# Sinkhorn-sorted attention into a squared-ReLU feed-forward layer: transposes in one bank for each moving engine, 1e-9 as a ninth row, and an earlier key move as the gate of w_in

## The chip, the cores and the metric

The kernel runs on one core of one Trainium2 chip. The time is device microseconds (us) of one execution, and the median over several executions is what counts. Before the change it is 230.9 us, the median of 6 runs that lie between 229.33 and 233.6 us.

A core has five engines with an instruction queue each, which run side by side and wait for one another through semaphores: PE (TensorE, matrix products and transposes; "PEld" is its loading of the stationary operand), DVE (VectorE), ACT (ScalarE), POOL (GpSimd) and SP (SyncE, which here only issues transfers). POOL issues transfers too. Each engine takes its own instructions strictly in the order of the program.

## The reference

The inputs are q, k and v (4 batches, 8 heads, 768 tokens, 64 dimensions), a sort net of 8x8 numbers for every batch and head, and a feed-forward layer's w_in (512x2048) and w_out (2048x512) with scalars s and b.

```python
P = sort_net
for _ in range(5):
    P = exp(P - max(P, axis=-1))
    P = P / (sum(P, axis=-1) + 1e-09)
    P = P / (sum(P, axis=-2) + 1e-09)
k_sorted = einsum('bhij,bhjcd->bhicd', P, k_blocks)   # v_sorted likewise
attn = softmax(q_blocks @ k_sorted_blocks^T / 8)      # within a block of 96 tokens
x = (attn @ v_sorted_blocks) as (3072 tokens, 512)
out = (s * relu(x @ w_in)**2 + b) @ w_out             # (3072, 512), fp32
```

So the five rounds of normalizing (the Sinkhorn stage) work on 32 matrices of 8x8, each of the 8 blocks of keys and values becomes a weighted sum of all 8, attention runs inside blocks, and then comes the layer that holds nearly all of the arithmetic.

## The kernel before, in words

**Tiling.** Tokens are handled in 8 groups of 384 (half a batch, four blocks of 96). Every group goes through `ffn1` (x by w_in, 16 column blocks of 128 taken two at a time, then ReLU on ACT and a square on DVE into the tile `gt`) and `ffn2` (`gt` by w_out). The order of all engines' work is written out by hand: a call of `ffn1` or `ffn2` is given `slots`, a dictionary that says which small pieces of the next group's attention are put between which of its matmuls. Negative slot numbers belong to `ahead`: with ahead=3 the first halves of the sums of column blocks 0, 1 and 2 (`part(i, (0, 1))`, L418 on, which need only the first two of the four 128-row slices of x) are done first, and slot i-3 runs just before the i-th of them. Slot ("pre", 1) runs on PE after the second half of block 1's sum.

**Start.** The Sinkhorn stage (L185 to L205) keeps its 32 matrices in the tile `sn`, one per partition, and is a chain of small DVE instructions with one exponential on ACT in every round: row sums (L195), reciprocal, product (L197), column sums (L200), in the first round alone 1e-9 added to them (L203, from the small tile `eps`, filled at L110), reciprocal (L204), product (L205). PE meanwhile does matmuls on zeros (`warm`, L157). Then `spread_p`, `take_p` and `build_pd` turn the result into weights for batch 0, and three `k_piece` (L249) and four `v_piece` (L300) sort the keys and values of batch 0: PE writes a piece into PSUM, and ACT ("A") or DVE ("D") moves it to SBUF by `evac` (L241). The three key pieces go into disjoint columns of `KS[0]`, by ACT, DVE and ACT.

**The gate of the weights.** w_in and w_out are loaded by POOL (`load_w`, L126, called at L473). In front of it stands a POOL copy of one column (L472) from the third key piece's part of `KS[0]` to the tile `ones`, which makes POOL wait until ACT has moved that piece. `load_w` issues six pieces of w_in at L131 (first columns 0 to 511 and 512 to 1023 of row slices 0 and 1, then columns 0 to 511 of slices 2 and 3), the second half of batch 0's queries (four transfers, L99), two pieces (columns 512 to 1023 of slices 2 and 3), eight more, and four of w_out (L147). POOL then does fills (L496 to L502), loads two scalars and, in `loads(1)` (L517), batch 1's keys, values and queries (L88, L99) and reorders the values (`vp`, L171). Batch 1's first value pieces on PE (L304, in `ffn2` of group 0) need these.

**Around the transposes.** For each pair of heads, `s_piece` makes scores, `p_piece` weighs the values and normalizes them into the tile `x` (reciprocal L361, product L362 on DVE). `t_piece` (L371) transposes x on PE for two pairs of heads into `tr`, a PSUM tile of one bank, and moves it into `xt`, the right operand of `ffn1`. The letters in `eng` say who moves: "D" is DVE alone, "AD" is ACT for the first two blocks of 96 tokens and DVE for the other two. For group 0, head pairs 0 and 1 are transposed at L490 with "AD", and pairs 2 and 3 as slot -2 of `ffn1(0)` (L551) with "D". `tr` comes from the pool `psb` with two banks, which are used in turn by the `warm` matmuls, `tr`, the query transposes `tqb` (L286, `q_blocks`) and the score banks `scb` (L334).

Of the kernel before, what the change touches and what calls it, by code (L numbers as in the profile page):

```python
# [9 lines left out]
FP = mybir.dt.float32  # L10
BF = mybir.dt.bfloat16
AF = mybir.ActivationFunctionType
ALU = mybir.AluOpType
# [3 lines left out]
def spread(t, dims):  # L17

    return bass.AP(tensor=t.tensor, offset=t.offset, ap=[list(t.ap[0])] + dims)
# [3 lines left out]
def kernel(  # L23
# [12 lines left out]
    nc = tc.nc  # L36

    B, H, S, D = q.shape
    NB = sort_net.shape[-1]
    BLK = S // NB  # L40
    BH = B * H
# [4 lines left out]
    HB = NB // 2  # L46
# [6 lines left out]
    CK = 16  # L53
# [5 lines left out]
    const = ctx.enter_context(tc.tile_pool(name="const", bufs=1))  # L59
# [9 lines left out]
    psb = ctx.enter_context(tc.tile_pool(name="psb", bufs=2, space=bass.MemoryType.PSUM))  # L69
    ctx.enter_context(tc.manual_schedule())  # L70


    sn = const.tile([BH, NB, NB], FP)
    nc.sync.dma_start(out=sn, in_=sort_net.rearrange("b h i j -> (b h) i j"))
    v0f = gtp.tile([128, C2, D], FP, tag="gt", name="v0f")
    CV = C2 // 4
    for c in range(0, C2, CV):
        nc.sync.dma_start(out=v0f[:, c:c + CV, :].rearrange("p c d -> p (c d)"),
                          in_=raw[2][0][:, c * D:(c + CV) * D])
# [13 lines left out]
    def load_q(b, ns=range(NB)):  # L93

        if b not in QTOK:
            QTOK[b] = rawp.tile([BLK, NB, H, D], BF, tag="rawq", name="qtok")
        qv = q[b].rearrange("h (n t) d -> t n h d", n=NB)
        for n in ns:
            nc.gpsimd.dma_start(out=QTOK[b][:, n], in_=qv[:, n])  # L99
# [5 lines left out]
    KS = [const.tile([128, NG, 2, GAP], BF, name=f"ks{i}") for i in range(2)]  # L105
    VS = [const.tile([KR, 2 * NG, VW], BF, name=f"vs{i}") for i in range(2)]
    nc.vector.memset(VP[0][:, :, C2:GAP], 0.0)
    nc.vector.memset(KS[0][:, :, :, C2:GAP], 0.0)
    eps = const.tile([BH, NB], FP)
    nc.vector.memset(eps, 1e-9)  # L110


    ident = const.tile([128, 128], BF)
# [8 lines left out]
    ones = const.tile([128, 32], BF)  # L122
# [3 lines left out]
    def load_w():  # L126
        wiv = moe_w_in.rearrange("(a p) f -> p a f", p=128)
        fq = d_ff // 4

        def part(a, f0, f1):  # L130
            nc.gpsimd.dma_start(out=wi[:, a, f0 * fq:f1 * fq], in_=wiv[:, a, f0 * fq:f1 * fq])  # L131

        for c in (0, 1):
            for a in (0, 1):
                part(a, c, c + 1)
        for c in (0, 1):
            for a in (2, 3):
                part(a, c, c + 1)
            if c == 0:
                load_q(0, range(HB, NB))  # L140
        for c in (2, 3):
            for a in range(NHP):
                part(a, c, c + 1)
        wov = moe_w_out.rearrange("(f p) n -> p f n", p=128)
        for c in range(4):
            fs = slice(c * (NF // 4), (c + 1) * (NF // 4))
            nc.gpsimd.dma_start(out=wo[:, fs, :], in_=wov[:, fs, :])  # L147
# [17 lines left out]
    def permute(eng, b, src, cs=slice(0, C2), ds=slice(0, D)):  # L165
        o = VP[b % 2][:, ds, cs]
        i = src[:, cs, ds].rearrange("p c d -> p d c")
        if eng is nc.scalar:
            eng.copy(out=o, in_=i)
        else:  # L170
            eng.tensor_copy(out=o, in_=i)  # L171


    rstat = const.tile([BH, NB], FP)
# [5 lines left out]
            out=jsel, in_=ident.rearrange("p (h j z) -> p j h z", h=H, j=NB), axis=AX.XY, op=ALU.add),  # L180
        lambda: nc.vector.tensor_reduce(
            out=bm.rearrange("p (e z a) -> p e z a", e=2, z=2),
            in_=idv.rearrange("p a e j z -> p e z a j"), axis=AX.X, op=ALU.add),
# [3 lines left out]
                            op=ALU.subtract)  # L187
    warm(138, 128)
    for it in range(5):
        nc.scalar.activation(out=sn, in_=sn, func=AF.Exp)  # L190
        if it >= 1:
            permute(nc.scalar, 0, v0f, slice((it - 1) * CV, it * CV))
        if it in (1, 2):
            idle[it - 1]()
        nc.vector.tensor_reduce(out=rstat, in_=sn, axis=AX.X, op=ALU.add)  # L195
        nc.vector.reciprocal(out=rrec, in_=rstat)
        nc.vector.tensor_tensor(out=sn, in0=sn, in1=rrec.broadcast_to([BH, NB, NB]), op=ALU.mult)  # L197
        if it == 4:
            break
        nc.vector.tensor_reduce(out=rstat, in_=sn.rearrange("p i j -> p j i"),  # L200
                                axis=AX.X, op=ALU.add)
        if it == 0:
            nc.vector.tensor_tensor(out=rstat, in0=rstat, in1=eps, op=ALU.add)  # L203
        nc.vector.reciprocal(out=rrec, in_=rstat)  # L204
        nc.vector.tensor_tensor(out=sn, in0=sn, in1=spread(rrec, [[0, NB], list(rrec.ap[1])]),  # L205
                                op=ALU.mult)
# [34 lines left out]
    def evac(eng, out, in_):  # L241
        if eng == "A":
            nc.scalar.copy(out=out, in_=in_)  # L243
        else:
            nc.vector.tensor_copy(out=out, in_=in_)  # L245
# [3 lines left out]
    def k_piece(b, c0, eng):  # L249
        src, mov, dst = RAW["k", b], PD[b], KS[b % 2]  # L250
        ps = psa.tile([128, CK, 2, NG], FP, tag="a", name="tp")
        for c in range(CK):
            for e in range(2):
                nc.tensor.matmul(out=ps[e * 64:(e + 1) * 64, c].rearrange("p z g -> p (z g)"),  # L254
                                 lhsT=src[:, c0 + c, :],
                                 rhs=mov[:, e].rearrange("p z g -> p (z g)"),
                                 start=True, stop=True)
        evac(eng, dst[:, :, :, c0:c0 + CK], ps.rearrange("p c z g -> p g z c"))
# [112 lines left out]
    def t_piece(b, half, hp2, eng):  # L371

        x = X[b, half]
        if hp2 == 0:
            XT[b * 2 + half] = xtp.tile([128, HB, NHP, BLK], BF, tag="xt", name="xt")
        tr = psb.tile([128, 1024], BF, tag="b", name="tr")
        for hp in (hp2, hp2 + 1):
            for n in range(HB):
                c0 = (n * 2 + hp % 2) * BLK
                nc.tensor.transpose(out=tr[:, c0:c0 + BLK],  # L380
                                    in_=x[:, n, hp * 128:(hp + 1) * 128],
                                    identity=ident[0:BLK, 0:BLK])
        n = HB // len(eng)
        for i, g in enumerate(eng):
            evac(g, XT[b * 2 + half][:, i * n:(i + 1) * n, hp2:hp2 + 2, :],
                 tr[:, i * n * 2 * BLK:(i + 1) * n * 2 * BLK].rearrange("p (n a c) -> p n a c",
                                                                        n=n, a=2))

    def t_dma(b, half):
        x = X.pop((b, half))  # L390
# [7 lines left out]
    def ffn1(t, slots, ahead=0):  # L398

        gt = gtp.tile([128, NF, TG], BF, tag="gt", name="gt")  # L400
        GT[t] = gt
        xt = XT[t]
        H1 = {}

        def part(i, hpl):
            if i not in H1:
                H1[i] = psa.tile([128, 2, 512], FP, tag="a", name="hps")
            for f in range(2):
                for hp in hpl:
                    fc = (2 * i + f) * 128  # L410
                    nc.tensor.matmul(out=H1[i][:, f, 0:TG], lhsT=wi[:, hp, fc:fc + 128],  # L411
                                     rhs=xt[:, :, hp, :],
                                     start=(hp == 0), stop=(hp == NHP - 1))

        for i in range(ahead):
            for p in slots.get(i - ahead, ()):
                p()
            part(i, (0, 1))  # L418
        for i in range(NF // 2):
            part(i, (2, 3) if i < ahead else range(NHP))  # L420
            for p in slots.get(("pre", i), ()):
                p()
            rt = rtp.tile([128, 2, TG], BF, tag="rt", name="rt")
            h = H1.pop(i)[:, :, 0:TG]
            nc.scalar.activation(out=rt, in_=h, func=AF.Relu)  # L425
            nc.vector.tensor_tensor(out=gt[:, 2 * i:2 * i + 2, :], in0=rt, in1=rt, op=ALU.mult)  # L426
            for p in slots.get(i, ()):
                p()
# [38 lines left out]
    warm(3)  # L467
    k_piece(0, 0, "A")
    k_piece(0, CK, "D")
    k_piece(0, 2 * CK, "A")  # L470

    nc.gpsimd.tensor_copy(out=ones[:, 0:1], in_=KS[0][:, 0, 0, 2 * CK:2 * CK + 1])  # L472
    load_w()  # L473
    v_piece(0, 0, "D")
    v_piece(0, CK, "A")
    q_piece(0, 0, "D")
# [11 lines left out]
    warm(1)  # L488
    Z.clear()
    t_piece(0, 0, 0, "AD")  # L490
    norm2()
    p_piece(0, 0, 3)
# [50 lines left out]
    def SB(b, h, i): return lambda: s_banks(b, h, i)  # L543
    def P(b, h, i): return lambda: p_piece(b, h, i)
    def TP(b, h, i, eng): return lambda: t_piece(b, h, i, eng)
    def TD(b, h): return lambda: t_dma(b, h)
    def PDB(b): return lambda: build_pd(b)
    def QB(b, n0, eng): return lambda: q_blocks(b, n0, eng)


    ffn1(0, {-2: [TP(0, 0, 2, "D")], ("pre", 1): [QB(0, HB, "D"), QB(0, HB + 2, "D")],  # L551
             2: [SB(0, 1, 0)], 3: [SB(0, 1, 1), P(0, 1, 0)], 4: [SB(0, 1, 2), P(0, 1, 1)],
             5: [SB(0, 1, 3), P(0, 1, 2)], 6: [TP(0, 1, 0, "D"), P(0, 1, 3)]}, ahead=3)
    ffn1(1, {-2: [TP(0, 1, 2, "D")], 1: [lambda: take_p(1, B - 1, PB), PDB(1)], 4: [PDB(2)],
# [10 lines left out]
    for b in range(B):  # L565
        n = b + 1
# [48 lines left out]
```

## Time and profile before

| | us |
|---|---|
| median of the runs shown (6) | 230.9 |
| lowest and highest of them | 229.33 and 233.6 |
| the profiled execution, its own time | 229.33 |
| its span, first to last instruction | 227.6 |
| PE busy in the span | 216.8 (95%) |
| DVE, ACT, POOL busy | 124.8, 98.9, 68.0 |
| bytes moved by DMA | 25.82 MB, mean 113 GB/s |
| mean granted PE clock | 0.998 of full |

The profile is of one execution. The time of an execution is its span and 1.7 us around it (229.33 - 227.6). A row of the timeline reads: start, length (us), engine, line, operation, output <- inputs by the program's names, how many instructions were put together, and in brackets how long the engine stood idle before and what ended that wait. In the chain of waits, which is followed back from the last instruction, a row is start, length and what the end of the kernel was waiting for at that time.

### The profile page before, as it was taken

Reading aid. Unit: us, or ns where it says so; the run is one execution under the profiler, and the core shown is the slowest. Engines: PE = TensorE matmul, PEld = TensorE weight load, DVE = VectorE, ACT = ScalarE, POOL = GpSimd, SP = SyncE. Lnnn points to the kernel's source line nnn. Section 1 sums busy time; section 2 is a strip of 40 time slices with the busy share of each in tenths; the row PEclk is TensorE's granted clock in tenths of the full one; section 3 lists DMA queues with packets and bytes.
Section 4 is the critical chain, followed back from the end, with each engine's and each line's share of the span. In section 5 each row is a group of like instructions: output and inputs, shape, how many; then the busy total and the mean of one; then the engine's idle time right before and its main releaser. Section 6 shows DMA issues by size and latency. Waiting matters only on the chain.

```text
span 227.6 us, 5807 instructions
## 1 busy us (share of the span) xinstructions
PE 216.8 (95%) x2532; PEld 133.1 (58%) x2554; DVE 124.8 (55%) x224; ACT 98.9 (43%) x127; POOL 68.0 (30%) x112
## 2 busy tenths in 40 slices
PE   8997799999999999999999999999999999999993
PEld 8886456655556556665555556655556556654452
DVE  6766467553547643489556733498557544441221
ACT  4967276564324316546234236627152246650000
POOL 8419689343900009291000018390000000000000
PEclk9999999999999999999999999999999999999999
DMA  6998999999951566994111568993123340001212
GB/s 185 233 74 95 170 184 189 206 199 156 129 145 46 118 161 119 192 158 90 49 46 59 151 120 164 176 168 48 49 95 58 107 115 3 1 0 46 94 49 92
DMA packets 53930, 25.82 MB, mean 113 GB/s; under 512 B 44944, under 2 KB 49296, under 8 KB 53904
## 3 DMA queue, kind: packets, MB, share of 16 engines
q0 software_dynamic: 30864, 12.85, 46.8%
q1 hardware_dynamic: 23040, 12.59, 22.0%
q8 instruction: 20, 0.33, 0.6%
q14 instruction: 6, 0.05, 0.1%
HBM read 27.27 MB, written 6.29 MB: 147 GB/s over the span
## 4 chain that ended last, share of the span: by engine, by line
PE 72%; DMA 11%; POOL 9%; DVE 3%; issue 3%; ACT 1%; POOLq 0%
PE ops L436 32%; PE hps L411 27%; DMA rawv<-in_v_dram 7%; PE pv L354 3%; POOL wi L131 3%; DMA wi<-in_moe_w_in_dram 3%; PE tv L304 2%; PE sc L319 2%; POOL vp L171 2%; PE tp L254 2%; PE ops L449 2%; POOL wo L147 1%; ACT ks L243 1%; DMA sn<-in_sort_net_dram 1%; ACT sn L190 1%
## 5 line engine op out<-in xcount | busy, mean ns | idle before, releaser
L411 PE MATMUL hps<-xt,wi 128*128 128x384 bf16 x512 | 85.7, 326 | 0.9 <-DVE xt L245 0.7
L436 PE MATMUL ops<-wo,gt 128*128 128x512 bf16 x348 | 81.6, 379 | 2.3 <-issue 1.9
L425 ACT ACTIVATE rt<-hps 128x768 bf16<-128x768 f32 x64 | 51.1, 811 | 56.7 <-PE hps L411 49.0
L426 DVE TENSOR_TENSOR gt<-rt 128x768 bf16<-128x768 bf16 x64 | 46.8, 738 | 41.6 <-ACT rt L425 40.9
L411 PEld LDWEIGHTS <-wi 128*128 128x128 bf16 x512 | 49.4, 98 | 34.1 <-issue 1.2
L436 PEld LDWEIGHTS <-gt 128*128 128x128 bf16 x368 | 33.7, 98 | 36.9 <-issue 0.6
L457 DVE SCALAR_TENSOR_TENSOR ot<-ops,s_bc,bias 128x512 f32<-128x512 f32 (+1 forms) x25 | 18.2, 730 | 30.9 <-PE ops L436 28.4
L324 ACT ACTIVATE at<-sc 112x768 bf16<-112x768 f32 x28 | 21.3, 808 | 30.2 <-PE sc L319 30.2
L99 POOL DMA_DIRECT2D qtok<-in_q_dram x32 | 24.9, 793 | 19.4 <-DMA rawv<-in_v_dram 9.0
L362 DVE TENSOR_TENSOR x<-pv,rec 96x512 bf16<-96x512 f32 x32 | 22.0, 686 | 1.1
L245 DVE CAST vs<-tv 112x1024 bf16<-112x1024 f32 x11 | 13.3, 1223 | 10.7 <-PE tv L304 10.6
L171 POOL COPY vp<-rawv 128x384 bf16<-128x384 bf16 x24 | 18.9, 840 | 0.0
L354 PEld LDWEIGHTS <-at 112*128 112x128 bf16 (+1 forms) x256 | 12.8, 101 | 6.7 <-ACT at L324 0.6
L561 POOL COPY gate<-gt 128x1 bf16<-128x1 bf16 x2 | 0.4, 191 | 54.2 <-DVE gt L426 54.2
L354 PE MATMUL pv<-vs,at 112*128 112x66 bf16 (+1 forms) x256 | 13.9, 195 | 0.6 <-DVE vs L245 0.5
L161 PE MATMUL z<-zeros 128*128 128x128 bf16 (+1 forms) x142 | 11.0, 247 | 1.2 <-DVE zeros L102 1.0
L304 PEld LDWEIGHTS <-vp 128*64 128x64 bf16 x512 | 9.1, 112 | 3.8 <-issue 2.5
L304 PE MATMUL tv<-pd,vp 128*64 128x64 bf16 x512 | 10.4, 197 | 0.6 <-POOL vp L171 0.3
L161 PEld LDWEIGHTS <-zeros 128*128 128x128 bf16 x144 | 10.0, 111 | 1.3 <-DVE zeros L102 1.0
L243 ACT CAST ks<-tp 128x1024 bf16<-128x1024 f32 x8 | 8.1, 1012 | 4.1 <-PE tp L254 4.0
L131 POOL DMA_DIRECT2D wi<-in_moe_w_in_dram x16 | 8.6, 547 | 2.4 <-DMA wi<-in_moe_w_in_dram 1.1
L243 ACT CAST vs<-tv 112x1024 bf16<-112x1024 f32 x5 | 5.1, 1018 | 9.6 <-PE tv L304 9.6
(77 smaller groups left out, 104.2 us busy)
## 6 DMA issues: line engine op xcount, KB each, us to landing
out_dram<-ot SPq DMA_DIRECT2D x23, 256.0 KB, 2.0
qtok<-in_q_dram POOLq DMA_DIRECT2D x32, 96.0 KB, 9.7
rawk<-in_k_dram POOLq DMA_DIRECT2D x3, 768.0 KB, 6.7
rawv<-in_v_dram POOLq DMA_DIRECT2D x3, 768.0 KB, 9.9
wi<-in_moe_w_in_dram POOLq DMA_DIRECT2D x16, 128.0 KB, 5.0
wo<-in_moe_w_out_dram POOLq DMA_DIRECT2D x4, 512.0 KB, 10.5
v0f<-in_v_dram SPq DMA_DIRECT2D x4, 384.0 KB, 4.6
rawk<-in_k_dram POOLq DMA_DIRECT2D x3, 256.0 KB, 9.3
```

The costliest lines, as they stand in the source:

```text
L99: nc.gpsimd.dma_start(out=QTOK[b][:, n], in_=qv[:, n])
L161: nc.tensor.matmul(out=Z[0][:, 0:w], lhsT=zeros[:, 0:128], rhs=zeros[:, 0:w], start=True, stop=True)
L171: eng.tensor_copy(out=o, in_=i)
L304: nc.tensor.matmul(out=ps[z * GAP:(z + 1) * GAP, d, :], lhsT=VP[b % 2][:, d0 + d, :], rhs=PD[b][:, :, z, :], start=True, stop=True)
L324: nc.scalar.activation(out=at, in_=sc[0:KR, :, 0:TG], func=AF.Exp, scale=scale)
L354: nc.tensor.matmul(out=pv[0:m, e, n * VW:(n + 1) * VW], lhsT=atf[:, c0:c0 + m], rhs=VS[b % 2][:, e * NG + g0 + n, :], start=True, stop=True)
L362: nc.vector.tensor_tensor(out=x[:, :, hp * 128:(hp + 1) * 128].rearrange("p n (e d) -> p e n d", e=2), in0=pvv[:, :, :, 0:D], in1=rec.unsq ...
L411: nc.tensor.matmul(out=H1[i][:, f, 0:TG], lhsT=wi[:, hp, fc:fc + 128], rhs=xt[:, :, hp, :], start=(hp == 0), stop=(hp == NHP - 1))
L425: nc.scalar.activation(out=rt, in_=h, func=AF.Relu)
L426: nc.vector.tensor_tensor(out=gt[:, 2 * i:2 * i + 2, :], in0=rt, in1=rt, op=ALU.mult)
L436: nc.tensor.matmul(out=ops, lhsT=gt[:, f, m * 128:(m + 1) * 128], rhs=wo[:, f, :], start=(f == 0), stop=(f == NF - 1))
L457: nc.vector.scalar_tensor_tensor(out=ot[:, ns], in0=ops, scalar=s_bc, in1=BIAS[0][:, ns], op0=ALU.mult, op1=ALU.add)
```

## The change

Three edits. In the Sinkhorn stage the tile gets a ninth row `sne[:, 8, :]` of 1e-9 and `sn` becomes a view of the first eight rows; the column sums at L200 go over nine rows in four of the rounds, and the addition at L203 and the tile `eps` go. In `t_piece` every engine that moves gets a `tr` tile, and so a bank, of its own, with the transposes of its blocks written just before its move; head pairs 2 and 3 of group 0 are moved by "AD" and run as slot -1 (before the third of the first halves) where they ran as slot -2 (before the second). The POOL copy and `load_w` stand before the third key piece, and the copy reads a column of the second piece, which DVE moves.

```diff
--- before.py
+++ after.py
@@ -70,7 +70,8 @@
     ctx.enter_context(tc.manual_schedule())
 
 
-    sn = const.tile([BH, NB, NB], FP)
+    sne = const.tile([BH, NB + 1, NB], FP)
+    sn = sne[:, 0:NB, :]
     nc.sync.dma_start(out=sn, in_=sort_net.rearrange("b h i j -> (b h) i j"))
     v0f = gtp.tile([128, C2, D], FP, tag="gt", name="v0f")
     CV = C2 // 4
@@ -106,8 +107,7 @@
     VS = [const.tile([KR, 2 * NG, VW], BF, name=f"vs{i}") for i in range(2)]
     nc.vector.memset(VP[0][:, :, C2:GAP], 0.0)
     nc.vector.memset(KS[0][:, :, :, C2:GAP], 0.0)
-    eps = const.tile([BH, NB], FP)
-    nc.vector.memset(eps, 1e-9)
+    nc.vector.memset(sne[:, NB, :], 1e-9)
 
 
     ident = const.tile([128, 128], BF)
@@ -197,10 +197,8 @@
         nc.vector.tensor_tensor(out=sn, in0=sn, in1=rrec.broadcast_to([BH, NB, NB]), op=ALU.mult)
         if it == 4:
             break
-        nc.vector.tensor_reduce(out=rstat, in_=sn.rearrange("p i j -> p j i"),
+        nc.vector.tensor_reduce(out=rstat, in_=sne.rearrange("p i j -> p j i"),
                                 axis=AX.X, op=ALU.add)
-        if it == 0:
-            nc.vector.tensor_tensor(out=rstat, in0=rstat, in1=eps, op=ALU.add)
         nc.vector.reciprocal(out=rrec, in_=rstat)
         nc.vector.tensor_tensor(out=sn, in0=sn, in1=spread(rrec, [[0, NB], list(rrec.ap[1])]),
                                 op=ALU.mult)
@@ -373,18 +371,17 @@
         x = X[b, half]
         if hp2 == 0:
             XT[b * 2 + half] = xtp.tile([128, HB, NHP, BLK], BF, tag="xt", name="xt")
-        tr = psb.tile([128, 1024], BF, tag="b", name="tr")
-        for hp in (hp2, hp2 + 1):
-            for n in range(HB):
-                c0 = (n * 2 + hp % 2) * BLK
-                nc.tensor.transpose(out=tr[:, c0:c0 + BLK],
-                                    in_=x[:, n, hp * 128:(hp + 1) * 128],
-                                    identity=ident[0:BLK, 0:BLK])
         n = HB // len(eng)
         for i, g in enumerate(eng):
+            tr = psb.tile([128, 1024], BF, tag="b", name="tr")
+            for hp in (hp2, hp2 + 1):
+                for m in range(n):
+                    c0 = (m * 2 + hp % 2) * BLK
+                    nc.tensor.transpose(out=tr[:, c0:c0 + BLK],
+                                        in_=x[:, i * n + m, hp * 128:(hp + 1) * 128],
+                                        identity=ident[0:BLK, 0:BLK])
             evac(g, XT[b * 2 + half][:, i * n:(i + 1) * n, hp2:hp2 + 2, :],
-                 tr[:, i * n * 2 * BLK:(i + 1) * n * 2 * BLK].rearrange("p (n a c) -> p n a c",
-                                                                        n=n, a=2))
+                 tr[:, 0:n * 2 * BLK].rearrange("p (n a c) -> p n a c", n=n, a=2))
 
     def t_dma(b, half):
         x = X.pop((b, half))
@@ -467,10 +464,10 @@
     warm(3)
     k_piece(0, 0, "A")
     k_piece(0, CK, "D")
+
+    nc.gpsimd.tensor_copy(out=ones[:, 0:1], in_=KS[0][:, 0, 0, CK:CK + 1])
+    load_w()
     k_piece(0, 2 * CK, "A")
-
-    nc.gpsimd.tensor_copy(out=ones[:, 0:1], in_=KS[0][:, 0, 0, 2 * CK:2 * CK + 1])
-    load_w()
     v_piece(0, 0, "D")
     v_piece(0, CK, "A")
     q_piece(0, 0, "D")
@@ -548,7 +545,7 @@
     def QB(b, n0, eng): return lambda: q_blocks(b, n0, eng)
 
 
-    ffn1(0, {-2: [TP(0, 0, 2, "D")], ("pre", 1): [QB(0, HB, "D"), QB(0, HB + 2, "D")],
+    ffn1(0, {-1: [TP(0, 0, 2, "AD")], ("pre", 1): [QB(0, HB, "D"), QB(0, HB + 2, "D")],
              2: [SB(0, 1, 0)], 3: [SB(0, 1, 1), P(0, 1, 0)], 4: [SB(0, 1, 2), P(0, 1, 1)],
              5: [SB(0, 1, 3), P(0, 1, 2)], 6: [TP(0, 1, 0, "D"), P(0, 1, 3)]}, ahead=3)
     ffn1(1, {-2: [TP(0, 1, 2, "D")], 1: [lambda: take_p(1, B - 1, PB), PDB(1)], 4: [PDB(2)],
```

## The prediction

> **What bounds the kernel now.** I read the page's shares first: PE is busy for 216.8 of 227.6 us, so what PE idles, some 10.8 us, is all that a change of order can win. Then the chain of waits, to see what sets the end before PE's own work does:
>
> ```profile
> 14.66 1.02 ACT ks L243
> ...
> 15.82 0.19 POOL ones L472
> ...
> 17.39 6.04 DMA wi<-in_moe_w_in_dram
> ...
> 38.77 16.66 DMA rawv<-in_v_dram
> ...
> 56.53 4.79 POOL vp L171 x6
> 61.32 0.04 issue
> 61.36 0.44 PE tv L304 x16
> ```
>
> From 61.4 us on the chain is PE to the end (0.48 us of DVE and the last store apart). Before it, it isn't PE: from the third key move (end 15.68) it runs through POOL's gate, w_in's pieces, POOL's list of issues, batch 1's values (landed 55.44) and their reordering. So PE's work between 16 and 61 us has slack against this chain. How much: batch 1's first 96 value matmuls take from 59.33 to 61.80, 2.47 us, and the same 96 in the next batch 1.64 (at 110.17 in the chain). So 0.83 us are lost there waiting for POOL.
>
> Next, the timeline of the places that the change touches, PE, ACT and DVE together:
>
> ```profile
> 22.20 0.50 PE L380 MATMUL tr<-ident,x 96*128 96x96 bf16 x8
> 22.74 0.48 ACT L243 COPY xt<-tr 128x384 bf16<-128x384 bf16 x1 [0.33 <-PE tr L380]
> 23.25 0.36 DVE L245 COPY xt<-tr 128x384 bf16<-128x384 bf16 x1 [1.24 <-ACT xt L243]
> 23.66 0.81 PE L411 MATMUL hps<-xt,wi 128*128 128x384 bf16 x4 [0.69 <-DVE xt L245]
> 25.33 0.34 PE L380 MATMUL tr<-ident,x 96*128 96x96 bf16 x4 [0.49 <-DVE x L362]
> 28.11 0.85 PE L286 MATMUL tqb<-ident,qtok 96*128 96x96 bf16 x16
> 29.30 0.66 PE L411 MATMUL hps<-xt,wi 128*128 128x384 bf16 x3 [0.18 <-DMA wi<-in_moe_w_in_dram]
> ```
>
> DVE's half of the move begins only when ACT's has ended, and PE idles 0.69 us for it; later 0.49 us for the last product of x. But the last row matters more: PE then stands still for a w_in piece. It is the eighth; it was issued at 24.36 and took 4.9 us, so it landed at 29.26. That transfer is on the POOL chain, so whatever PE wins before 29.3 is lost again there unless the transfer moves too.
>
> **Part 1, the ninth row.**
>
> ```profile
> 3.81 0.25 DVE L200 TENSOR_REDUCE rstat<-sn 32x8 f32<-32x64 f32 x1
> 4.10 0.15 DVE L203 TENSOR_TENSOR rstat<-rstat,eps 32x8 f32<-32x8 f32 x1
> 4.29 0.19 DVE L204 RECIPROCAL rrec<-rstat 32x8 f32<-32x8 f32 x1
> ```
>
> Removing L203 takes 4.29 - 4.10 = 0.19 us out of a chain in which every instruction waits for the one before. Four column sums get 8 more elements each. No row has 72 elements; the sums over 64 and over 192 elements (0.22 us for PT of batch 0, 0.35 for PT of batches 1 to 3) give (0.35 - 0.22)/128 = 1.0 ns an element, so 8 ns, four times 0.03 us. From both sides: 0 if a short instruction's fixed cost hides them, 4 x 0.25 x 8/64 = 0.12 if the time is in proportion; I take 0.03, since the two rows bracket 72. The fill at 2.17 stays where it was. If it now had to wait for sort_net's landing (2.29) because it writes into the same tile, its 0.07 us would come on the path; its row is disjoint from what the transfer writes, so I take 0, at most 0.1. Net 0.16 us earlier, range 0 to 0.19. ACT is no bound here: a round lasts 1.76 us (4.76 to 6.52) and ACT's exponential and value copy take 1.69 of it (4.76 to 6.45). Everything after the stage moves by 0.16, PE's zero matmuls having ended at 10.63, before the stage does (11.0).
>
> **Part 2, the gate.** The second key move is a DVE row from 14.16 for 1.23 us and ends at 15.39; the third, ACT's, ends at 15.68. POOL has been idle for 7.52 us before its copy, so the copy and all behind it move by 0.29 us. Nothing is queued behind the waiting copy on POOL but these issues, and SP isn't touched. That earlier transfers start at once is seen in the one-microsecond windows (last columns: granted clock, DMA share, GB/s):
>
> ```profile
> 14.00:15.00 1.00, 0.91 (x59) 0.82 (x54) 0.84 (x1) 1.00 (x2) 0.00 (x0) 1.00 0.34 22
> 16.00:17.00 1.00, 1.00 (x35) 0.88 (x29) 0.72 (x2) 0.83 (x1) 0.71 (x3) 1.00 0.00 0
> ```
>
> The DMA engines run dry before w_in, so the whole list (w_in, queries, w_out, keys, values) begins 0.16 + 0.29 = 0.45 us earlier and, being one stream in a fixed order, should land 0.45 earlier.
>
> Two things could spoil it. First, the third key move could have to wait for POOL's copy, if reading one column of the tile blocked writing others: it would start at 15.72, not 14.66, so up to 1.06 us on ACT. Against it, ACT and DVE moved key pieces into interleaved columns of that tile at the same time (13.65 to 15.68 and 14.16 to 15.39). I take 0; PE's slack before 29.3 (below) would hide most of it. Second, a rule of the Trainium skill speaks against an earlier issue: by "SBUF — State Buffer", section "Who interferes with whom", a DVE copy in a two-port mode locks GpSimd out of a port pair that it needs to write descriptors, and GpSimd then waits for all of that instruction. The first w_in issue, before at 16.30, would come at 15.85, within the DVE value cast that ran from 15.45 to 16.68. If that blocked, the issue would come at 16.68 - 0.16 = 16.52, and the change would cost 0.22 us in place of winning 0.45. The rows say no: the six issues of 16.30 to 19.5, alongside DVE moves out of PSUM at 15.45, 16.95 and 18.39, took 0.56 to 0.58 us each, against 0.53 later with a quieter DVE. So at most 0.05 each, and those exist already. I take 0.45, between -0.22 and 0.45.
>
> **Part 3, the transposes.** The eight transposes stay, as four and four, and so do 0.48 us of ACT. DVE's move starts when the second four are done, at 22.74 beside ACT's instead of at 23.25: 0.51 earlier (0 if the two are kept apart by writing the same xt, but their parts of it are disjoint). PE's first sums start at 23.15, DVE's next products end at 23.93 and 24.77 where they ended at 24.44 and 25.28. With the second transposes moved behind two first halves, PE does 8 sums in a row at 0.173 us (16 in 2.77), waits 0.1 for the bank of the product that ends at 23.93, and comes to the transposes at about 24.65, so their 0.49 us wait falls to 0.1. Their move, 0.56 us of DVE alone, is 0.48 of ACT beside 0.36 of DVE, under the 0.7 us of the third first half. The query transposes, which began at 28.11, could begin at 27.15: PE wins 0.96 us.
>
> And it goes away at once. The last of the queries issued at 21.79 takes 6.2 us and lands at 28.0, the seventh and eighth w_in pieces at 28.6 and 29.26. Less the gate's 0.29 (on a clock that leaves out part 1), PE waits 0.2 for queries, 0.2 for the seventh and 0.3 for the eighth piece, until 28.97. So at the row that was at 29.30, PE is earlier by 0.29 + 0.16 = 0.45, the POOL chain's shift, and not by 0.96 + 0.16. The score matmuls behind it took 0.42 us to the next row (29.89 to 30.31) where the like ones take 0.27 (31.72 to 31.99), waiting for DVE's query moves, which now come earlier: 0.15 more, PE ahead by 0.60. That also is spent, at 59.33, where the values come only 0.45 earlier.
>
> **Sum.** 0.16 + 0.29 + 0 = 0.45 us on the path. The profiled execution's own 229.33 (span 227.6 and 1.7 around it) becomes 228.9. It was the fastest of the six; the same 0.45 off the median 230.9 gives 230.4. One per cent, 2.3 us, is about what a measurement of this kernel can tell from no change, its runs lying 4.3 us apart, so this forecast is "the same".
>
> **The rivals.**
> *More comes through* (0.20): the transfers land earlier by more than the gate moved, so PE keeps its 0.60 and the 0.83 us wait at 59.33 vanishes: 1.43 us off, 229.5. For it: the landing of the values is 16.66 us of shared transfer, in which a shift can grow. Against it: same list, same order, same queue.
> *The transfers hide the change* (0.12): w_out and the values come at the rate of the DMA engines and land when they did; then both PE gains wait, 230.9. For it: the DMA digits are 9 from 11 to 57 us. Against it: the windows above.
> *PE's clock drops* (0.18, slower): PE's waits for queries and w_in now lie together, about 0.7 us between 27.5 and 29. By the Trainium skill, "TensorE: Matmul & The Clock Gate", section "HAM oscillation — how this bites in real kernels", a gap that fills an idle window of about 3.4 us halves the clock. Such a window at half speed costs some 1.7 us: 230.4 + 1.7 = 232.1, two 233.8. [...]The trace is against it: from 23 to 24 us PE was busy for 0.34 us and the granted clock stayed 1.00; by the row the price is 0.
>
> **The numbers.** My forecast has 0.50; its own range is 229.1 to 231.7, from the part bounds and medians of such scattered runs. Of it I leave 0.08 to faster by over 1% (under 228.6) and 0.05 to slower by over 1% (over 233.2); of "more comes through" 0.10 and 0.01; of "hide" 0.02 and 0.01; of the clock, half, 0.09, to slower. That makes faster 0.20, same 0.64, slower 0.16. The range that leaves out two in ten reaches to both rivals: 228.4 to 232.8.
>
> **What would show it.** After, the chain should still pass from POOL's copy to the values, at about 15.4 in place of 15.8, and the values land near 55.0. ACT's and DVE's xt moves should overlap, PE's first sums start near 23.0, and PE should wait for w_in at about 28.85, longer than 0.2 us. No L203 row. I am wrong if PE no longer waits for w_in or vp, if the copy at L472 still comes at 15.8, if issues on POOL grow past 0.58 us, or if the granted clock falls below 1.00 before 62 us.

## The result and the profile after

The changed kernel took 231.40 us (median of 35 runs, 229.56 to 233.43), the kernel before 231.16 us (72 runs, 229.09 to 234.38) in the same sessions. The ratio is 1.0019, 95% interval [1.0003, 1.0035]: 0.4 us slower, where 0.45 us faster was forecast. It is within 1% of no change, as forecast, but the sign is not. (The medians are of all runs; the ratio is of the means of those runs that lie within 1.5% of the fastest of their kernel.)

The profiled execution of the changed kernel took 232.44 us, with a span of 230.7 us against 227.6. Its chain of waits (start, length, what was waited for) runs through the same places, but begins elsewhere:

```profile
2.14 7.28 DMA v0f<-in_v_dram
...
9.44 1.51 ACT vp L169
10.95 0.17 ACT sne L190
...
16.34 0.19 POOL ones L468
...
40.23 18.33 DMA rawv<-in_v_dram
...
59.66 4.75 POOL vp L171 x6
...
64.45 0.44 PE tv L302 x16
```

Two things are to be seen. The third quarter of batch 0's values (v0f) landed at 9.41; before, it landed at 7.1 (issued at 2.13, 5.0 us). ACT's cast of it stands in front of the fifth exponential, which therefore came at 10.86 and not at 9.89 (10.05 before, less the 0.16 of the ninth row). The Sinkhorn stage ended 0.80 us later than before (the first product on `pe` at 11.96, not 11.16), and POOL's copy came at 16.34, not 15.82, though the gate's own gain was there (0.28 us: DVE's key piece ended at 16.20, ACT's at 16.48). Then the stretch from that copy to the first reordering of batch 1's values (vp) took 59.66 - 16.34 = 43.32 us; before it took 56.53 - 15.82 = 40.71. The differences, 0.52 and 2.61, add up to the 3.1 us between the spans.

The sums over nine rows, in the timeline of DVE, are as forecast: 0.30 us from the first sum to the reciprocal, where it was 0.48 with the addition between.

```profile
3.80 0.27 DVE L200 TENSOR_REDUCE rstat<-sne 32x8 f32<-32x72 f32 x1
4.10 0.19 DVE L202 RECIPROCAL rrec<-rstat 32x8 f32<-32x8 f32 x1
```

The transposes, in the timelines of ACT, DVE and PE:

```profile
23.07 0.48 ACT L241 COPY xt<-tr 128x384 bf16<-128x384 bf16 x1 [0.17 <-PE tr L380]
23.29 0.36 DVE L243 COPY xt<-tr 128x384 bf16<-128x384 bf16 x1 [0.77 <-PE tr L380]
23.79 1.55 PE L408 MATMUL hps<-xt,wi 128*128 128x384 bf16 x8 [0.27 <-DVE rec L359]
25.18 0.62 PE L380 MATMUL tr<-ident,x 96*128 96x96 bf16 x8
28.85 0.34 PE L284 MATMUL tqb<-ident,qtok 96*128 96x96 bf16 x4 [0.34 <-DMA qtok<-in_q_dram]
30.39 1.13 PE L408 MATMUL hps<-xt,wi 128*128 128x384 bf16 x4 [1.20 <-DMA wi<-in_moe_w_in_dram]
```

ACT and DVE move at the same time (before, DVE waited for ACT), PE's wait ahead of the first sums is 0.27 us in place of 0.69, and the wait for x at the second transposes is gone. What PE won it gave back three rows further down: 0.34 us for queries and 1.20 for w_in.

### The profile page after: what moved, and what is told of

It is laid out like the page before. It is cut to its first block, busy times and chain, and to the rows that moved or that the text cites. A ratio compares the mean times of both kernels' runs of the same rounds, so it can differ in the third digit from the quotient of the medians.

```text
span 230.7 us, 5809 instructions
## 1 busy us (share of the span) xinstructions
PE 217.8 (94%) x2532; PEld 133.6 (58%) x2554; DVE 124.7 (54%) x223; ACT 99.5 (43%) x128; POOL 67.9 (29%) x112
## 4 chain that ended last, share of the span: by engine, by line
PE 71%; DMA 16%; POOL 7%; issue 2%; DVE 1%; ACT 1%; SPq 1%; POOLq 0%
PE ops L433 32%; PE hps L408 27%; DMA rawv<-in_v_dram 8%; DMA wi<-in_moe_w_in_dram 5%; DMA v0f<-in_v_dram 3%; PE pv L352 3%; PE tv L302 2%; PE sc L317 2%; POOL vp L171 2%; PE tp L252 2%; PE ops L446 2%; POOL wo L147 1%; POOL wi L131 1%; ACT vp L169 1%; DVE ks L243 1%
## 5 line engine op out<-in xcount | busy, mean ns | idle before, releaser
L302 PE MATMUL tv<-pd,vp 128*64 128x64 bf16 x512 | 10.7, 197 | 1.6 <-POOL vp L171 1.4
L241 ACT CAST vs<-tv 112x1024 bf16<-112x1024 f32 x5 | 5.1, 1018 | 10.7 <-PE tv L302 10.7
```

The lines of the kernel that those rows point to most:

```text
L302: nc.tensor.matmul(out=ps[z * GAP:(z + 1) * GAP, d, :], lhsT=VP[b % 2][:, d0 + d, :], rhs=PD[b][:, :, z, :], start=True, stop=True)
```

## The experiments

Each ratio is to the kernel before, run on the same chip in the same session. First the three edits one by one, and the gate moved further; then the gate far forward and far back, and the change repeated; then combinations; last four kernels without half of w_out, in which batch 1's values can't bind.

**e1, the ninth row alone**

```diff
-    sn = const.tile([BH, NB, NB], FP)
+    sne = const.tile([BH, NB + 1, NB], FP)
+    sn = sne[:, 0:NB, :]
...
-        if it == 0:
-            nc.vector.tensor_tensor(out=rstat, in0=rstat, in1=eps, op=ALU.add)
```

> The kernel before with the ninth row alone. Theory A (the Sinkhorn chain of DVE sets its own end): 0.16 us off, ratio 0.9993. Theory B (the third and fourth quarters of batch 0's values land late, ACT's cast waits for them and the next exponential waits behind the cast): nothing, ratio 1.000, and the profile shows ACT waiting for v0f before L169. Theory C (the tile's new layout in SBUF harms): slower, 1.002.

Measured: 0.9986 [0.9964, 1.0008], which leaves out C (1.002) and doesn't tell A from B. ACT waited for no quarter of the values in its profile. Its profile showed a mask that no theory had named. In PE's timeline the zeros' matmuls last 10.72 us (9.63 before), and the first product of `pe` follows them without a wait:

```profile
1.01 10.72 PE L161 MATMUL z<-zeros 128*128 128x128 bf16 x138 [1.01 <-DVE zeros L103]
11.65 1.10 PE L215 MATMUL pe<-sne,emat 32*128 32x64 f32 x8
```

The stage itself was done near 10.9 here; PE's filling work held the chain until 11.65.

**e2, the gate on the second key piece alone**

```diff
-    k_piece(0, 2 * CK, "A")
 
-    nc.gpsimd.tensor_copy(out=ones[:, 0:1], in_=KS[0][:, 0, 0, 2 * CK:2 * CK + 1])
+    nc.gpsimd.tensor_copy(out=ones[:, 0:1], in_=KS[0][:, 0, 0, CK:CK + 1])
     load_w()
+    k_piece(0, 2 * CK, "A")
```

> The kernel before with only the gate of w_in moved to the second key piece. If the transfers from w_in to batch 1's values move with the gate: 0.29 us off, ratio 0.9987. If what holds the end lies elsewhere, or the earlier issue is paid for by slower landing: 1.000 to 1.002.

Measured: 1.0008 [0.9985, 1.0030]. The copy came at 15.58, 0.24 earlier than before, and the values' reordering at 59.15, 2.6 later. Not decisive for so small a step.

**e3, the transposes alone**

```diff
-        tr = psb.tile([128, 1024], BF, tag="b", name="tr")
...
         for i, g in enumerate(eng):
+            tr = psb.tile([128, 1024], BF, tag="b", name="tr")
...
-    ffn1(0, {-2: [TP(0, 0, 2, "D")], ("pre", 1): [QB(0, HB, "D"), QB(0, HB + 2, "D")],
+    ffn1(0, {-1: [TP(0, 0, 2, "AD")], ("pre", 1): [QB(0, HB, "D"), QB(0, HB + 2, "D")],
```

> The kernel before with only the transposes changed (a bank for each moving engine, head pairs 2 and 3 by both engines at slot -1). By the prediction PE wins 0.96 us and loses it at the wait for the eighth piece of w_in, so 0, ratio 1.000. If the change as a whole is slow through PE's waits: 1.001 to 1.003.

Measured: 0.9995 [0.9973, 1.0018], so nothing, as forecast. But something came with it that was not forecast. PE waited 0.47 us for queries and 1.40 for w_in, and behind these waits its granted clock fell (windows of 2 us: PE busy, number of matmuls, granted clock, DMA share, GB/s):

```profile
28.00:30.00 2.00, 0.34 (x4) 1.00 1.07 139
30.00:32.00 2.00, 1.82 (x14) 0.84 1.23 201
32.00:34.00 2.00, 2.00 (x7) 0.50 1.16 185
34.00:36.00 2.00, 2.00 (x24) 0.81 0.77 98
```

In 9 of the 22 executions of e3 the mean granted clock is 0.990 to 0.993; their median is 232.74 us, that of the other 13 is 230.35. Of the kernel before, 10 of 72 executions in the same session have such a clock, of e1, e2 and e4 together 8 of 66.

**e4, the gate on the first key piece** (else as before)

```diff
     k_piece(0, 0, "A")
+    nc.gpsimd.tensor_copy(out=ones[:, 0:1], in_=KS[0][:, 0, 0, 0:1])
+    load_w()
     k_piece(0, CK, "D")
```

> The kernel before with the gate of w_in on the first key piece, which ACT ends about 1.0 us before the third: the suspected effect of the gate about three times as large. If the transfers move with the gate and the end with them: 1.0 us off, ratio 0.9957, until PE itself holds (0.83 us of value wait are there to win). If an earlier issue costs, slower than the second-piece gate: 1.002 or more.

Measured: 0.9978 [0.9954, 1.0001], 0.5 us off. The interval leaves out a loss (1.002) and reaches both the forecast gain (0.9957) and, at its other end, no change. A larger step was needed.

**e5, the gate on the mixing weights**

```diff
     build_pd(0)
+    nc.gpsimd.tensor_copy(out=ones[:, 0:1], in_=PD[0][:, 0, 0, 0:1])
+    load_w()
     pe = spread_p(1, B - 1)
```

> The kernel before with the gate of w_in on batch 0's mixing weights (the tile pd, ready at 12.86 us before), 2.9 us earlier than the third key piece. If the values of batch 1 land as much earlier as the gate moves, as long as the DMA engines are free (they run dry at about 14.2 us): 1.8 to 2.9 us off, ratio 0.987 to 0.992. If the stream's length from gate to values grows as the gate comes earlier: 1.000 or slower.

Measured: 0.9872 [0.9829, 0.9914], some 3 us off, and its six runs lie between 228.56 and 229.24 us, where the kernel before spreads over 4. In its timelines (POOL, then PE) the copy is at 13.35, the values' reordering begins 5.4 us before PE asks for it, and PE's first 96 value matmuls run in 1.71 us without a wait:

```profile
13.35 0.19 POOL L465 COPY ones<-pd 128x1 bf16<-128x1 bf16 x1 [5.03 <-DVE pd L235]
53.95 6.42 POOL L171 COPY vp<-rawv 128x384 bf16<-128x384 bf16 x8
```

```profile
59.37 1.71 PE L304 MATMUL tv<-pd,vp 128*64 128x64 bf16 x96
```

**e6, the gate on the second value piece** (written behind `v_piece(0, CK, "A")`)

```diff
+    nc.gpsimd.tensor_copy(out=ones[0:KR, 0:1], in_=VS[0][:, 0, CK:CK + 1])
+    load_w()
     q_piece(0, 0, "D")
```

> The kernel before with the gate of w_in on the second value piece, which ACT ends at 17.2 us before, 1.5 us later than the third key piece. If the values land as much later: 1.5 us more, ratio 1.0065. If the gate's place doesn't matter because the stream is held by something else: 1.000.

Measured: 1.0056 [1.0032, 1.0080], 1.3 us more for a gate 1.5 us later. Together with e5 this shows that the values' landing moves with the gate, and the end with it until PE binds. How nearly one to one, two profiles can't tell: from e5 to e6 the copy is 4.33 us later and the reordering 6.78.

**e7 and e12, the changed kernel again**, with no edit.

> The changed kernel once more. If its 1.0019 is a loss of its own: 1.001 to 1.004 again. If it is the scatter of the stream from gate to values, with the predicted gain of 0.45 us or a part of it behind it: 0.998 to 1.001. The span should again be the start of the reordering of batch 1's values and 171.05 us.

> The changed kernel a third time, since its first two ratios, 1.0019 and 0.9963, exclude each other. If both are scatter about a gain of 0.29 to 0.45 us: 0.996 to 1.001; if the first is the true one: 1.001 to 1.004.

Measured: 0.9963 [0.9939, 0.9987] and 1.0010 [0.9982, 1.0039]. The second of the three measurements excludes the first. Weighted by runs (35, 22, 22) the mean is 1.0001. So the loss of the first measurement is not a property of the change that repeats; nor is a gain of 0.2% shown.

**e8, the ninth row without its masks**

```diff
-    warm(138, 128)
+    warm(118, 128)
...
-        if it >= 1:
+        if it in (1, 2):
...
+    for c in (2, 3):
+        permute(nc.scalar, 0, v0f, slice(c * CV, (c + 1) * CV))
```

> The ninth row alone, with what can hide its 0.16 us taken away: the casts of the third and fourth quarters of batch 0's values stand behind the last exponential, and 118 matmuls on zeros run in place of 138. If these two masks hold the end of the Sinkhorn stage in some executions (0.8 us by the late quarter in the changed kernel's profile, 0.6 us by the zeros in the ninth row's): 0.2 to 0.5 us off, ratio 0.998 to 0.999. If not: 0.9993, as with the ninth row alone.

Measured: 0.9960 [0.9932, 0.9988], 0.9 us off: more than the forecast, of which 0.998 lies inside the interval. The third quarter landed late here too (2.14 and 6.6 us, so 8.7), and the fifth exponential did not wait for it; `pe` began at 11.03. The interval overlaps e1's, and the two masks were taken away together, so the share of each stays open. In 8 of the 22 executions the granted clock is 0.983 to 0.993, in e1 in 2 of 22.

**e9, the changed kernel with the gate on the mixing weights**: the last two edits and the row of the change, with e5's gate.

> The changed kernel with the gate on the mixing weights, so that batch 1's values no longer set the end. If the change's PE gains are real and only hidden behind the stream of transfers: 0.9 to 1.1 us below the kernel before with that gate (0.9872), ratio 0.982 to 0.984. If the change has a loss of its own: not below 0.987.

Measured: 0.9811 [0.9763, 0.9858], 227.64 us, the fastest of all, which leaves out the loss that the expectation set against the gain (0.987). In its PE timeline neither queries nor w_in hold PE any more, and the sums that began at 28.84 in e5 begin at 27.61:

```profile
26.92 0.84 PE L284 MATMUL tqb<-ident,qtok 96*128 96x96 bf16 x16
27.61 0.82 PE L408 MATMUL hps<-xt,wi 128*128 128x384 bf16 x4
```

Four of its six runs took 227.2 to 227.7 us, two 230.6 and 230.9. The last has a granted clock of 0.985; the other, at 0.997, is not explained. The interval overlaps e5's; the profiled spans are 225.8 and 226.8 us.

**e10, the same without the ninth row**

> The kernel before with the gate on the mixing weights and the changed transposes, without the ninth row. If the transposes' 0.96 us reach the end once w_in and the values come in time: 0.983; if the queries or the eighth piece of w_in still hold PE: 0.985 to 0.987.

Measured: 0.9836 [0.9786, 0.9886], which holds both forecasts. In the profiled execution the sums began at 27.75, so PE's gain is there without the row; but the values came at 56.23 and PE waited for them again.

**e11, e9 with e8's two edits**

> As the changed kernel with the gate on the mixing weights, and 118 matmuls on zeros in place of 138 and the casts of the third and fourth quarters of the values behind the last exponential. If PE's zeros hold the end of the Sinkhorn stage in about a third of the executions (10.5 us and more in three of ten profiles, where 9.3 to 9.9 leave room): 0.2 to 0.4 us below that kernel and narrower scatter, 0.981 to 0.983.

Measured: 0.9953 [0.9924, 0.9982], 2.9 us slower than e9 (0.981 to 0.983 was forecast). PE stood 1.68 us before `pe`, then 1.61 us in the middle of a run of value matmuls, with no other engine named ("issue"), and its granted clock fell. PE's windows (PE busy, granted clock, DMA share, GB/s):

```profile
18.00:20.00 2.00, 0.74 (x34) 1.00 0.99 122
20.00:22.00 2.00, 1.03 (x26) 0.87 1.65 178
22.00:24.00 2.00, 1.67 (x23) 0.50 2.24 171
24.00:26.00 2.00, 1.73 (x27) 0.78 1.30 152
```

The first sums came at 25.83, against 23.08 in e9. What the 1.61 us waited for stays open. The fall is no accident of this execution: 21 of the 22 have a granted clock of 0.971 to 0.993, and the one at 1.00 took 228.59 us, where the median is 230.5. Of e11's two edits, the 20 matmuls fewer lengthen PE's wait before `pe`; that they alone bring the fall is not shown.

**f1 to f4, half of w_out left out.** The edit, on the kernel before (f1), the changed kernel (f2), the changed kernel with the gate back on the third key piece (f3), and e1 (f4):

```diff
-        for c in range(4):
+        for c in range(2):
...
-                                 rhs=wo[:, f, :], start=(f == 0), stop=(f == NF - 1))
+                                 rhs=wo[:, f % 8, :], start=(f == 0), stop=(f == NF - 1))
```

> The kernel before with the second half of w_out left out (two of four transfers; the first eight slices of w_out are used in place of the last eight as well), so that the stream in front of batch 1's values is 2 MB shorter and the values should come before PE asks for them. All else as before. If the values' landing makes the scatter of 4 us: the median falls by 1.5 to 3 us, 0.987 to 0.993, and its runs lie within about 1 us.

> The changed kernel with the same half of w_out left out. If the prediction's steps up to the eighth piece of w_in hold (0.45 us there, 0.60 behind the score banks) and only the values hide them: 0.45 to 0.60 us below the kernel before cut in the same way. If the change wins nothing even where the values come in time: equal.

> As the changed kernel cut in that way, with the gate back on the third key piece, so the ninth row and the transposes alone. If w_in's eighth piece holds PE and moves with the gate: 0.29 us above it. If the gate's move wins nothing: equal.

> The kernel before cut in that way with the ninth row alone. If the row's 0.16 us come through: 0.16 us below the cut kernel before. If PE's zeros or the late quarters of the values hide them in many executions: 0 to 0.1.

Measured, in medians: f1 229.38 us (8 runs, seven of them within 229.14 to 229.98), f2 228.99 (6), f4 229.10 (6), f3 230.65 (21 runs in two groups, 9 of 228.7 to 229.8 and 12 of 230.3 to 231.6). f2 lies 0.39 us under f1 and f4 0.28 under it. f3's two groups are told apart by the clock: the faster nine have a granted clock of 0.997 to 1.00, and of the slower twelve eleven have 0.990 to 0.993. At full clock f3's median is 229.14 us (10 executions), 0.18 above f2's 228.96 (0.29 was forecast for the gate) and 0.05 above f4. But f3 and f4 differ by the transposes alone, and f3's median is 1.55 us higher: while none of f4's 6 executions has such a clock, and one of f1's 8, 11 of f3's 21 have. The row that binds is the one that the prediction named, the sums that wait for the eighth piece of w_in, here in the PE timelines of f1 and of f2:

```profile
30.03 0.66 PE L411 MATMUL hps<-xt,wi 128*128 128x384 bf16 x3 [0.99 <-DMA wi<-in_moe_w_in_dram]
```

```profile
29.82 0.66 PE L408 MATMUL hps<-xt,wi 128*128 128x384 bf16 x3 [1.10 <-DMA wi<-in_moe_w_in_dram]
```

The span is this start and 197.4 us in all four (227.4 - 30.03; 227.2 - 29.82; 227.5 - 30.09; 227.4 - 29.99). With the values out of the way most of the forecast gain is therefore seen in the medians (0.39 of 0.45 to 0.60; 0.21 between the two rows), though so few runs, spread over 1.9 to 2.9 us, don't share it out between the edits.

## Why the prediction was right or wrong

**One row for every profile with all of w_out.** The table sets the copy at the gate beside the start of batch 1's reordering (vp) and the span, in us.

| kernel | gate copy | vp starts | between | span | span - vp start |
|---|---|---|---|---|---|
| before | 15.82 | 56.53 | 40.7 | 227.6 | 171.1 |
| changed | 16.34 | 59.66 | 43.3 | 230.7 | 171.0 |
| e7, changed again | 15.61 | 58.20 | 42.6 | 229.2 | 171.0 |
| e12, changed again | 15.44 | 59.97 | 44.5 | 233.2 | 173.2 |
| e1 row | 16.35 | 58.16 | 41.8 | 229.2 | 171.0 |
| e2 second piece | 15.58 | 59.15 | 43.6 | 230.2 | 171.1 |
| e3 transposes | 15.99 | 58.77 | 42.8 | 229.9 | 171.1 |
| e4 first piece | 14.90 | 57.66 | 42.8 | 228.7 | 171.0 |
| e6 value piece | 17.68 | 60.73 | 43.1 | 231.7 | 171.0 |
| e8 row unmasked | 15.69 | 57.27 | 41.6 | 228.3 | 171.0 |
| e9 changed, weights | 13.09 | 54.80 | 41.7 | 225.8 | 171.0 |
| e10 transposes, weights | 13.24 | 56.23 | 43.0 | 227.2 | 171.0 |
| e5 weights | 13.35 | 53.95 | 40.6 | 226.8 | 172.9 |
| e11 all unmasked | 12.89 | 54.73 | 41.8 | 228.4 | 173.7 |

*What bounds the kernel* was right: except where PE binds (e5, e11) or its clock falls behind the values (e12, below), the span is the values' arrival and 171.0 us, whatever stands before. But the column "between" goes from 40.6 to 43.6 (44.5 in e12) with the same transfers in the same order, and the kernel before had been profiled in an execution at the short end. That it lost only 0.83 us to the wait for the values was luck: in the changed kernel's profile the 96 value matmuls, which take 1.64 us, went on from 60.77 to 64.90, for 4.13.

*Part 1, the ninth row.* The 0.16 us on DVE were nearly right: in the changed kernel's profile the fourth exponential came at 8.13 and not 8.29; in e1 the fifth came at 9.92 and not 10.05, 0.13 earlier (the sums over 72 elements took 0.27 to 0.28 us in the profiles of the changed kernel, some 0.02 above the 0.25 to 0.26 before, where 0.008 was taken). What failed is what stood beside it: "ACT is no bound here" and "PE's zero matmuls having ended at 10.63, before the stage does". Both were read off one execution. ACT's cast can wait for a quarter of the values (0.97 us in the changed kernel's profile), and the zeros last from 9.3 to 10.7 us from profile to profile; in e1, e5, e6 and e9 `pe` followed them with no wait. In such an execution little or nothing of the 0.16 arrives. Over the profiles with 138 matmuls on zeros `pe` starts at 11.16 to 11.48 without the row (eight, median 11.34) and at 11.07 to 11.96 with it (eight, median 11.23).

*Part 2, the gate.* The 0.29 us are in the profile, neither of the two dangers came (ACT moved the third piece without a gap, 2.02 us for two; POOL's six issues took 3.24 us, 3.23 before), and e5 and e6 show that the landing follows the gate. What failed is the step "should land 0.45 earlier", taken as a difference that a measurement would show with its sign: it is a seventh of the 3 us by which the stream's length varies. Whether the landing did move by 0.45 is therefore not shown. In the four profiles with the gate on the second piece the stream took 42.6 to 44.5 us, in the four with it on the third 40.7 to 42.8; single executions can't tell a loss from scatter here, and e2's time (1.0008, at most 1.0030) leaves no room for a loss of the 1.8 us between these means.

*Part 3, the transposes.* Right in what the traces show: moves side by side, first sums 0.67 earlier against the stage (23.66 + 0.80 - 23.79; forecast 0.51), and PE's gain lost at the queries and at w_in. The 0.96 us exist: once w_in comes in time, e9 has its sums at 27.61 where e5 has 28.84, of which 0.22 is the earlier start of `pe` (11.25 against 11.47). But a gain that is lost at a wait makes the wait longer, and this was not free.

*PE's clock: the step that failed.* The prediction named this rival and then put it at nothing: "by the row the price is 0", a row of one execution. The profiled execution of the changed kernel does have a granted clock of 1.00 throughout, but not every execution has. Each one on record has a mean granted clock of 0.993 or less, or of 0.997 or more, and the two kinds lie some 2 us apart:

| kernel | executions | with 0.993 or less | their median, us | median of the others, us |
|---|---|---|---|---|
| before, in the experiments | 202 | 39 (19%) | 233.37 | 231.03 |
| changed (result, e7, e12) | 80 | 30 (38%) | 232.72 | 230.76 |
| e3, transposes | 22 | 9 | 232.74 | 230.35 |
| f1 and f4, without the transposes | 14 | 1 | 231.44 | 229.34 |
| f3, with them | 21 | 11 | 231.02 | 229.14 |

(Three executions of the kernel before, of 322 us and more, are left out. In the sessions of e7 and e12 alone it is 18 of 44 against 22 of 102; for the kernel before in the result's session no clocks are on record.) So the change makes falls of the clock about twice as frequent. An estimate from this table: 18 points more of some 2.0 us are 0.36 us, against a forecast gain of 0.45. (It takes the clock as the whole difference between the two kinds; longer waits may have a part in it.) Over all executions in the table both kernels have the same mean, 231.5 us.

e3's profile shows one such fall, where the rival had it: PE's waits, before three that stood apart (0.69, 0.49 and 0.18 us), have become 0.47 and 1.40 within 2.3 us, and the clock behind them is short by (0.16 + 0.50 + 0.19) x 2 = 1.7 us, the prediction's own price. In that execution the wait for the values still hid it (span - vp start is 171.1). In e12's it was not hidden: there the clock fell from 62 to 70 us, behind the wait for the values, to 0.70, 0.50, 0.50 and 0.59, and 15 matmuls by w_out took 5.36 us where the changed kernel's first profile has 3.40. f3, in which the values come 5.9 us before PE asks for them, points to the waits for queries and w_in. Two things stay open. Where the falls lie in the executions without a profile is not on record. And the waits alone don't decide: in the changed kernel's profile (0.34 and 1.20 us), in f3's (1.53 and 0.18) and at that place in e12's (0.45 and 1.37) no fall followed.

*The sum.* In f1 and f2 it is 0.39 us (forecast 0.45 to 0.60 there). In the whole kernel three measurements gave 1.0019, 0.9963 and 1.0010, a mean of 1.0001, where 0.998 was forecast. So two terms of the sum "0.16 + 0.29 + 0" failed: the 0 for the transposes has no price for the clock, which costs an estimated 0.36 us, and the 0.45 us is less than the stream's own scatter, so that a single measurement could miss its sign. Why the first was slower by more than its interval is shown only in part: 8 of the 31 runs that its ratio takes in have a clock of 0.993 or less, and without them their mean is 231.06 us in place of 231.32, against 230.87 for the kernel before; the 0.19 us left lie within the scatter. Of the signs of being wrong that the prediction gave, the late copy came in the first profile (16.34, for the late quarter of the values) and the clock below 1.00 before 62 us in e3's. Of the rivals, "PE's clock drops" (0.18) has the mechanism that the runs show, though in a part of the executions and not in all; its 232.1 us is near the median of the changed kernel's slower kind, 232.7.

## What to carry to other kernels

When the end hangs on the landing of one transfer, work out how long its stream takes in several profiles before trusting a gain of tenths: here the stream scattered over 3 us and the gain was 0.45. Look for the step that moves the whole stream out of the binding place: a gate whose copy came 2.5 us earlier (13.35, not 15.82) was worth 1.3%, and let the transposes' gain, worth nothing on its own, get past w_in. Read every "ends before" of a profile with its margin: 0.4 us of margin was not kept by matmuls that only fill time, nor 1.3 us (7.1 against the cast at 8.45) by a transfer. And look at the granted clock of every execution, not of the profiled one: an edit that closes small waits of PE in front of a fixed landing gathers them into one, and here the falls of the clock became twice as frequent.

## What the runs showed of the hardware

138 matmuls on zeros took 9.31 to 10.72 us in kernels with the same code for them. A transfer of 384 KB issued at 2.14 us landed after 4.4 to 7.3 us. A gap of 1.68 us and one of 1.61 us some 7 us later (e11, PE half busy behind it), and gaps of 0.47 and 1.40 us within 2.3 us (e3), were followed by a granted clock down to 0.50; gaps of 0.34 and 1.20 us (changed kernel) and of 0.71 us (e8) were not. In e3 and in e11 the clock was short by 1.7 us in all, as much as 3.4 us at half speed, and in e12 by 3.4 us, twice that.
